# A fused linear-attention and gated-convolution kernel: the first two batches in a hand-written order

## The chip, the cores and the metric

The kernel runs on one core of one Trainium2 chip. Time is device time in microseconds, the median of the runs. A core has five engines that work beside each other: TensorE (PE; its weight loads are shown as PEld), VectorE (DVE), ScalarE (ACT), GpSimd (POOL) and SyncE (SP). Each takes its own instructions in order. Data moves between DRAM and the on-chip memory (SBUF) through 16 DMA engines; matmuls write into a small accumulator memory (PSUM).

## The reference

There are 8 batches, 8 heads, a sequence of 576 and a head dimension of 64. The first half is a linear attention with cosine weights over the position, the second a projection, a long convolution done with a Fourier transform, a product of three terms and an output projection.

```python
q_p, k_p = phi(q), phi(k)       # phi(x) = concat(relu(x) * cos_w, relu(x) * sin_w)
kv  = einsum('bhsf,bhsd->bhfd', k_p, v);  z = sum(k_p, axis=2)
num = einsum('bhsf,bhfd->bhsd', q_p, kv)
den = einsum('bhsf,bhf->bhs', q_p, z)[..., None] + 1e-06
x   = (num / den) with the heads side by side             # (8, 576, 512)
x1, x2, x3 = split(x @ w_proj, 3)                          # w_proj: 512 x 1536
x2_conv = irfft(rfft(x2, axis=1) * rfft(filter_fft, axis=0))
out = (x1 * x2_conv * x3) @ w_out                          # float32
```

## The kernel before

One batch goes through these stages; a name in brackets is the tile that the stage writes, and appears so in the profile.

- `load_qk` reads q, k and v of a batch from DRAM as fp32 and writes them to SBUF as fp16 (`raw`, six buffers in turn; 512 KB and 64 KB for each of q, k, v). GpSimd issues these loads, and those of the weights `wp`, `wo` and of the filter `filt`.
- `emit_phi` makes phi(k) (`kp`) and phi(q) (`qp`) on VectorE (lines 107 and 109, which are helpers). `emit_va` copies v (`va`), on ScalarE (L149) or VectorE.
- `emit_kv` multiplies kp and va on PE (L435) and copies the result (`kvs`).
- `emit_qt` transposes qp into `qpt`. For batches 0 and 1 PE does it, and ScalarE and VectorE each copy one head (L459, L460). From batch 2 on it is four DMA transposes per batch issued by SyncE (L447). There is one `qpt` buffer, so that the transposes of a batch wait for `num` of the batch before.
- `emit_num` multiplies qpt and kvs (L472), and VectorE divides (`rcp`, then `att`, L482).
- `emit_fx` is the first step of the Fourier transform, a matmul over att (L499, L505), copied to `fx` (L510). `emit_xt` transposes att into `xt`: by PE for batch 0, by one DMA transpose on SyncE (L520) for the others.
- `emit_gate` multiplies xt with two thirds of w_proj (L604: 64 matmuls per batch in four chunks), ScalarE copies the two results (L609), VectorE multiplies them (`g`).
- `emit_x2` multiplies fx with the other third (L541, `x2f`), `emit_dft` does the second step of the transform (L580, `xf`) and the product with the filter's spectrum on VectorE (`m`, `yf`), `emit_inv` goes back (L621, L625, `eq`), `emit_y` combines (`eo`, `y`, `ye`), and `emit_out` makes the output (L671, L677), which ScalarE copies (`os`) and SyncE writes to DRAM (L704, L692).

Before batch 0 the kernel makes its tables: GpSimd writes counters (`emit_iotas`), VectorE turns them into columns (`emit_cols`, `emit_rows`), ScalarE takes sines of them (`emit_fwd_tables`, `emit_inv_turns`, `emit_inv_tables`, `emit_h_tables`), and PE makes the filter's spectrum (`emit_h`: hE, hO, hL). `warm_up` issues matmuls whose result is not used.

Batches overlap: a step of the loop `for b in range(1, B + 1)` has x2, dft, gate and inv of batch b, num and fx of batch b+1, the loads of batch b+2, and out of batch b-1. Source order is not the order on the engines: a planner reorders the instructions of each engine, by its own costs and by when buffers come free, and `with behind(key)` puts the instructions of its block behind a marked instruction on the same engine. In the order that it settled on, SyncE issues the transposes `qpt` of batch 2, `xt` of batch 1, `qpt` of batch 3, `xt` of batch 2, the output of batch 0, `qpt` of batch 4, `xt` of batch 3, the output of batch 1, and so on.

Of the kernel before, what the change touches and what calls it, by code (L numbers as in the profile page):

```python
# [17 lines left out]
def kernel(  # L18
# [19 lines left out]
    nc = tc.nc  # L38
# [58 lines left out]
    feo = setupp.tile([NP, 2, 3, DM], FP16, tag="feo", name="feo")  # L97
    qpt_buf = const("qpt", [128, NH, SP_], FP16)
# [33 lines left out]
    def load_qk(b, nm, hs=slice(0, NH)):  # L132
        src = {"q": q, "k": k, "v": v}[nm]
        if hs.start == 0:
            raw_t[(b, nm)] = raw_buf[raw_n[0] % len(raw_buf)]
            raw_n[0] += 1
        rw = raw_t[(b, nm)]
        nc.gpsimd.dma_start(  # L138
            out=rw[:, hs, 0 : 4 * D],
            in_=src[b, hs, 0:NM].rearrange("h (p j) d -> p h (j d)", j=4),  # L140
        )
        nc.gpsimd.dma_start(
            out=rw[0:64, hs, 4 * D : 5 * D], in_=src[b, hs, NM:S].rearrange("h p d -> p h d")
        )

    def emit_va(b, xs=range(4), copy=nc.scalar.copy):
        for x in xs:
            hs = slice(2 * x, 2 * x + 2)
            copy(  # L149
                out=va_buf[b % 2][:, hs, :, 0:D],  # L150
                in_=raw_t[(b, "v")][:, hs].rearrange("p h (j d) -> p h j d", j=NJ),
            )

    def emit_input_dma(b):
        load_qk(b, "q")
        load_qk(b, "k")
        load_qk(b, "v")
# [23 lines left out]
    def emit_iotas(part):  # L181
        if part == 0:
            iota("s4_i", [128, NJ], lambda t: [
                (t[:, 0:4], [[1, 4]], 0, 4), (t[0:64, 4:5], [[1, 1]], NM, 1),
                (t[64:128, 4:5], [[1, 1]], 0, 1),
            ])
            iota("p_i", [128, 1], lambda t: [(t, [[1, 1]], 0, 1)])
            iota("kr_i", [128, 4, 2], lambda t: [(t, [[1, 4], [0, 2]], 1, 0)])
            iota("nrow_i", [128, 128], lambda t: [(t, [[1, 128]], 0, 0)])
            iota("er_i", [128, 4, 16], lambda t: [(t, [[1, 4], [4, 16]], 0, 0)])  # L190
            return
# [11 lines left out]
    def emit_cols():  # L203
# [7 lines left out]
        for r in raw_buf[0:3]:  # L211
            nc.vector.memset(r[64:128, :, 4 * D : 5 * D], 0.0)
# [32 lines left out]
        for r in raw_buf[3:]:  # L245
            nc.vector.memset(r[64:128, :, 4 * D : 5 * D], 0.0)
# [56 lines left out]
    def emit_fwd_tables():  # L303
# [14 lines left out]
        frac(tn)  # L318
        sin_of(fsin, tn[:, 0:288])
# [9 lines left out]
    def emit_inv_tables():  # L329
        tn, mk = cc["tn_inv"], cc["mk"]  # L330
        frac(tn)
        sin_of(itab[:, 3:6].rearrange("p a b -> p (a b)"), tn[:, 0 : 3 * QS])
        cos_of(itab[:, 0:3].rearrange("p a b -> p (a b)"), tn[:, QS : 4 * QS])
        for c in range(NC):
            for par in range(2):
                tsc(itl[:, c, :, par], itab[:, 2:4], mk[:, 2 * c + par : 2 * c + par + 1], AL.mult)

    def emit_h_tables():
# [8 lines left out]
        tnf = tn.rearrange("p a b -> p (a b)")  # L347
        frac(tnf)
        sin_of(hs_.rearrange("p a b -> p (a b)"), tnf)
        cos_of(hc.rearrange("p a b -> p (a b)"), tnf)  # L350

        hb = cc["hb"] = setupp.tile([NP, 3, 3, 32], FP16, tag="hb", name="hb")
# [6 lines left out]

    def emit_h(bls):  # L360
        hc, hs_, hb = cc["hc"], cc["hs"], cc["hb"]
        fa = filt16.rearrange("p x (j n) -> p x j n", j=3)
        for x, op in ((0, AL.add), (1, AL.subtract)) if 0 in bls else ():
            with behind("phi", 1, "k"):
                nc.vector.tensor_tensor(
                    out=feo[:, x].rearrange("p j n -> p (j n)"),
                    in0=filt16[:, 0], in1=filt16[:, 1], op=op,
                )
# [29 lines left out]
    def emit_phi(b, nm, h0=0, nh=NH):  # L398
        rw = raw_t[(b, nm)]
        dst = kp_t if nm == "k" else qp_t  # L400
        if nm == "k":
            if h0 == 0:
                dst[b] = work.tile([128, NJ, NH, 2, D], FP16, tag="kp", bufs=1, name=f"kp{b}")
            t = dst[b]
            for j in range(NJ):
# [37 lines left out]
    def emit_qt(b, hp):  # L443
        qp, qpt = qp_t[b], qpt_buf
        hsl = slice(2 * hp, 2 * hp + 2)
        if b >= DMA_QT:
            nc.sync.dma_start_transpose(  # L447
# [5 lines left out]
        for hh in range(2):  # L453
            for j in range(NJ):
# [3 lines left out]
                )  # L458
        nc.scalar.copy(out=qpt[:, 2 * hp], in_=u[:, 0, 0:SP_])  # L459
# [29 lines left out]
    def emit_fx(b, cs=range(NC), wm=0):  # L489
# [4 lines left out]
        for c in cs:  # L494
# [15 lines left out]
            mark["fx", b] = nc.scalar.copy(  # L510
# [52 lines left out]
    def emit_dft(b, bls=range(3)):  # L563
# [6 lines left out]
        for bl in bls:  # L570
# [11 lines left out]
            mark["xf", b, bl] = nc.scalar.copy(out=xf, in_=u[:, :, 0:n])  # L582
            m1 = work.tile([128, 2, n], FP16, tag=f"m1{n}", bufs=1, name=f"m1_{b}_{bl}")
# [10 lines left out]
    def emit_gate(b, c):  # L594
        xt = xt_t[b]
        if c == 0:
            moe.setdefault(b, {})["g"] = work.tile([128, NC, S], FP16, tag="g", name=f"g{b}")
# [113 lines left out]
    HA, HB = slice(0, 4), slice(4, 8)  # L711
    load_qk(0, "k", HA)
    emit_iotas(0)
    for nm, hs in (("v", HA), ("q", HA), ("k", HB), ("v", HB), ("q", HB)):
        load_qk(0, nm, hs)
    emit_iotas(1)
    load_wp(0)
    load_wp(2)
    load_wp(1)
    load_qk(1, "q")  # L720
    load_qk(1, "k")
    load_qk(1, "v")
    load_filter()
    load_wo()
    emit_cols()
    emit_warm(1)
    emit_phi(0, "k", 0, 4)
    emit_va(0, (0, 1))
    emit_kv(0, 0)
    emit_phi(0, "q", 0, 4)  # L730
    for hp in (0, 1):
        emit_qt(0, hp)
    emit_num(0, 0, 4)
    emit_num(0, 1, 1)
    emit_phi(0, "k", 4, 4)
    emit_va(0, (2, 3))
    emit_kv(0, 1)
    emit_fx(0, (0, 1))
    emit_xt(0, (0, 1))
    emit_phi(0, "q", 4, 4)  # L740
    for hp in (2, 3):
        emit_qt(0, hp)
    emit_num(0, 2, 1)
    emit_num(0, 3, 1)
    emit_xt(0, (2, 3))
    emit_fx(0, (2, 3), 3)
    emit_rows()
    emit_inv_turns()
    for c in range(NC):
        emit_gate(0, c)  # L750
    emit_fwd_tables()
    with behind("att", 0, 3):
        emit_phi(1, "q")
    for hp in range(4):
        emit_qt(1, hp)
    emit_h_tables()
    with behind("g", 0, 0):
        emit_phi(1, "k")
    with behind("x0s", 0, 2):
        emit_va(1)  # L760
    emit_x2(0, (0,))
    emit_kv(1)
    emit_x2(0, (1,))
    emit_num(1, 0)
    emit_num(1, 1)
    emit_x2(0, (2,))
# [3 lines left out]
    emit_h((0,))  # L770
    emit_dft(0, (0,))
    emit_h((1,))
    emit_dft(0, (1,))
    emit_h((2,))
    emit_dft(0, (2,))
    with behind("kvs", 1):
        emit_inv_tables()
    emit_input_dma(2)
    with behind("qpt", 1, 3):
        emit_phi(2, "q")  # L780
    with behind("att", 1, 1):
        emit_phi(2, "k")
    with behind("x2f", 0, 2):
        emit_va(2)
    for c in range(NC):
        emit_qt(2, c)
    for c in range(NC):
        emit_fx(1, (c,))
    setup_stack.close()
    late["p"] = ctx.enter_context(tc.tile_pool(name="late", bufs=1))  # L790
    emit_x2(1, (0, 1))
    for c in range(NC):
        emit_inv(0, c)
    emit_kv(2)

    for b in range(1, B + 1):
# [16 lines left out]
        if b == 1:  # L813
            for c in range(NC):
                emit_y(0, c)
# [20 lines left out]
        if n + 1 < B:  # L836
            emit_input_dma(n + 1)
            with behind(*(("yf", 0, 2) if b == 1 else ("g", b - 1, NC - 1))):
# [3 lines left out]
            with behind(*("att", n, 3)):  # L842
                emit_phi(n + 1, "k")
            if b == 1:
                with behind("kvs", 2):
                    emit_va(n + 1)
            else:
                with behind("eo", b, 3):
                    emit_va(n + 1, (0, 1))
                with behind("g", b, 0):  # L850
                    emit_va(n + 1, (2, 3), nc.vector.tensor_copy)
# [42 lines left out]
```

## Time and profile before

| | us |
|---|---|
| median of 3 runs (254.1 to 255.73) | 255.11 |
| the profiled execution, its own time | 254.64 |
| its span in the profile | 252.9 |
| PE busy in the span | 216.1 (85%) |
| VectorE busy | 192.7 (76%) |
| ScalarE busy | 168.8 (67%) |
| mean granted PE clock | 0.941 of full speed |

The profile's times are counted from the start of the span. A group of instructions is shown with its line, engine, operation, the tile written and the tiles read, and a count (x40). An engine is idle until a releaser lets it go on: an instruction of another engine, or the landing of a DMA transfer. The granted PE clock is the speed that PE's throttle allows, 1.00 or about half. The DMA share is the mean busy share of the 16 DMA engines; it goes above 1 where packets overlap. "SPq" is SyncE's time on a DMA issue, which is not the time that the data takes: the time to landing is shown apart.

### The profile page before, as it was taken

To read this page: it belongs to the slowest core of one execution; us is meant where nothing else is said; L and a number is where in the kernel's file an instruction comes from. 1 tells how busy PE (TensorE), PEld (TensorE's weight loads), DVE (VectorE), ACT (ScalarE), POOL (GpSimd) and SP (SyncE) were. 2 spreads that over 40 slices of the span, in tenths; PEclk is the share of its full clock that TensorE was granted. 3 is DMA by queue.
4 is the path that set the end of the run, shared out by engine and by line. 5 is a ranking of instruction groups with operands and counts; after the bars stand their busy time and mean duration, and the time that the engine had idled before them with its cause. 6 is when DMAs were issued, how large, how long until landed. Compare 5 with 4: busy or idle time off the path is not lost.

```text
span 252.9 us, 5925 instructions
## 1 busy us (share of the span) xinstructions
PE 216.1 (85%) x2278; PEld 144.4 (57%) x2278; DVE 192.7 (76%) x660; ACT 168.8 (67%) x264; POOL 49.4 (20%) x79
## 2 busy tenths in 40 slices
PE   0379799989421899999999999999999999999980
PEld 0358577556210586668557855776586658635830
DVE  7589868799819159897979798978996694727751
ACT  2246999997512377478858876796679577767821
POOL 8992364523220002202220220000000000000000
PEclk9995999999755699999999999999999999999998
DMA  5999999999999999999999999965940531053015
GB/s 60 148 194 203 191 205 192 192 173 133 175 140 179 178 150 196 255 135 163 171 278 166 184 158 274 194 136 186 210 108 0 189 83 23 14 177 141 25 25 187
DMA packets 95613, 39.13 MB, mean 155 GB/s; under 512 B 63648, under 2 KB 91296, under 8 KB 95584
## 3 DMA queue, kind: packets, MB, share of 16 engines
q0 software_dynamic: 40064, 16.85, 54.6%
q1 hardware_dynamic: 55152, 21.31, 45.7%
q10 hardware_dynamic: 368, 0.59, 0.7%
q8 instruction: 18, 0.29, 0.5%
q14 instruction: 11, 0.09, 0.1%
HBM read 33.69 MB, written 9.44 MB: 171 GB/s over the span
## 4 chain that ended last, share of the span: by engine, by line
PE 64%; DMA 19%; ACT 9%; DVE 4%; POOL 2%; issue 1%; ACTq 0%; POOLq 0%
PE x L604 23%; PE out L671 11%; PE x L541 10%; DMA xt<-att 7%; DMA raw<-in_v_dram 5%; DMA qpt<-qp 4%; PE dft L580 4%; PE fx L499 3%; PE inv L621 3%; PE kv L435 3%; PE inv L625 3%; DMA raw<-in_k_dram 3%; ACT x2f L559 2%; DVE kp L109 2%; PE out L677 2%; PE fx L505 1%
## 5 line engine op out<-in xcount | busy, mean ns | idle before, releaser
L604 PE MATMUL x<-xt,wp 128*128 128x288 f16 x512 | 68.9, 291 | 5.9 <-DMA xt<-att 5.9
L604 PEld LDWEIGHTS <-wp 128*128 128x128 f16 x512 | 50.1, 99 | 21.4 <-DMA xt<-att 6.8
L541 PE MATMUL x<-wp,fx 128*128 128x512 f16 (+1 forms) x160 | 35.7, 388 | 0.8 <-DVE qpt L460 0.6
L559 ACT ACTIVATE x2f<-x 128x1024 f16<-128x1024 f32 (+1 forms) x24 | 21.0, 881 | 21.7 <-PE x L541 21.7
L671 PE MATMUL out<-wo,y 128*128 128x512 f16 x128 | 29.6, 379 | 2.5 <-ACT os L699 2.5
L611 DVE TENSOR_TENSOR g<-x0s,x2s 128x576 f16<-128x576 f16 x32 | 14.5, 453 | 20.5 <-ACT x2s L609 20.3
L609 ACT CAST x2s<-x 128x576 f16<-128x576 f32 x32 | 20.5, 640 | 11.3 <-PE x L604 11.3
L609 ACT CAST x0s<-x 128x576 f16<-128x576 f32 x32 | 20.6, 645 | 10.8 <-PE x L604 9.2
L482 DVE TENSOR_TENSOR att<-num,rcp 128x640 f16<-128x640 f32 x32 | 26.2, 822 | 0.6
L472 PE MATMUL num<-kvs,qpt 128*128 128x65 f16 x320 | 15.1, 198 | 10.7 <-DMA qpt<-qp 7.6
L472 PEld LDWEIGHTS <-qpt 128*128 128x128 f16 x320 | 13.0, 100 | 17.3 <-DMA qpt<-qp 8.6
L582 ACT CAST xf<-dft 128x1024 f16<-128x1024 f32 (+1 forms) x24 | 19.1, 802 | 4.8 <-PE dft L580 4.1
L541 PEld LDWEIGHTS <-fx 128*128 128x128 f16 (+1 forms) x160 | 12.6, 100 | 16.0 <-issue 3.3
L510 ACT CAST fx<-fx 128x576 f16<-128x576 f32 x32 | 20.3, 653 | 1.4 <-PE fx L505 1.4
L149 ACT COPY va<-raw 128x640 f16<-128x640 f16 x24 | 16.6, 746 | 6.2 <-DMA raw<-in_v_dram 6.2
L671 PEld LDWEIGHTS <-y 128*128 128x128 f16 x128 | 12.2, 98 | 14.2 <-issue 1.1
L138 POOL DMA_DIRECT2D raw<-in_k_dram x9 | 8.6, 954 | 52.9 <-DVE kp L109 50.2
L642 DVE TENSOR_TENSOR eo<-eq 128x288 f16<-128x288 f16 x64 | 17.7, 299 | 1.3 <-ACT eq L631 1.2
L631 ACT CAST eq<-inv 128x576 f16<-128x576 f32 x32 | 18.3, 672 | 0.0
L435 PE MATMUL kv<-va,kp 128*128 128x65 f16 x320 | 12.6, 198 | 6.1 <-ACT va L149 6.1
L702 ACT ACTIVATE os<-out 128x1024 f32<-128x1024 f32 x14 | 14.6, 1039 | 4.9 <-PE out L671 4.1
L109 DVE TENSOR_SCALAR kp<-raw,ccol 128x512 f16<-128x512 f16 (+1 forms) x45 | 16.9, 376 | 1.2 <-DMA raw<-in_k_dram 1.2
(154 smaller groups left out, 400.3 us busy)
## 6 DMA issues: line engine op xcount, KB each, us to landing
out_dram<-os SPq DMA_DIRECT2D x30, 256.0 KB, 3.4
raw<-in_q_dram POOLq DMA_DIRECT2D x7, 512.0 KB, 13.5
raw<-in_k_dram POOLq DMA_DIRECT2D x7, 512.0 KB, 13.4
raw<-in_v_dram POOLq DMA_DIRECT2D x7, 512.0 KB, 15.9
wp<-in_moe_w_proj_dram POOLq DMA_DIRECT2D x3, 512.0 KB, 8.6
out_dram<-os SPq DMA_DIRECT2D x15, 64.0 KB, 3.8
filt<-in_moe_filter_fft_dram POOLq DMA_DIRECT2D x2, 288.0 KB, 12.8
raw<-in_k_dram POOLq DMA_DIRECT2D x2, 256.0 KB, 5.3
```

What stands on the lines that cost most here:

```text
L109: return nc.vector.tensor_scalar(out=out, in0=in0, scalar1=s1, scalar2=s2, op0=op0, op1=op1)
L435: nc.tensor.matmul(u[:, h // 4, ds((h % 4) * 65, 65)], kp[:, j, h].rearrange("p a b -> p (a b)"), va[:, h, j, 0:65], start=(j == 0), stop= ...
L472: nc.tensor.matmul(u[:, hh, ds(t * 65, 65)], qpt_buf[:, h, ds(t * 128, 128)], kvs[:, h // 4, ds((h % 4) * 65, 65)], start=True, stop=True,)
L482: mark["att", b, hp] = nc.vector.tensor_tensor(out=att[:, hp].rearrange("p t (h d) -> p h t d", h=2), in0=nv[:, :, :, 0:D], in1=rcp.unsque ...
L510: mark["fx", b] = nc.scalar.copy(out=fx[:, c].rearrange("p (v t a) -> p t v a", t=4, a=16), in_=uf.rearrange("p (t v a) -> p t v a", t=4, ...
L541: nc.tensor.matmul(dst, fx[:, c, ds(128 * ch, n)], wp16[:, c, ds(DM, DM)], start=(c == cs[0]), stop=(c == cs[-1]),)
L559: mark["x2f", b, bl] = nc.scalar.mul(out=x2f[:, 2 * bl : 2 * bl + n], in_=u[:, 0:n], mul=X2SC)
L582: mark["xf", b, bl] = nc.scalar.copy(out=xf, in_=u[:, :, 0:n])
L604: nc.tensor.matmul(u[:, hf, 0:HS], wp16[:, i, ds(w * DM + c * 128, 128)], xt[:, i, ds(HS * hf, HS)], start=(i == 0), stop=(i == NC - 1),)
L609: mark[f"x{w}s", b, c] = nc.scalar.copy(out=x, in_=u[:, :, 0:HS])
L631: mark["eo", b, c] = nc.scalar.copy(out=eq.rearrange("p a b c -> p a (b c)"), in_=u[:, :, 0:HS])
L671: nc.tensor.matmul(u[:, x], y[:, c, ds(QS * t, 128)], wo16[:, c], start=(c == 0), stop=(c == NC - 1),)
```

## The change

Everything from the first instruction to `emit_kv(3)` is put between `manual_schedule()`'s enter and exit; in this stretch each engine gets its instructions in source order, and the source is a long list of calls written out by hand. The loop then starts at b = 2, and the special cases for b = 1 in it are gone. Many helpers are split, so that their VectorE and ScalarE parts can be placed apart (`emit_h_tables`, `emit_h_sines`, `emit_h_left`, `emit_feo`, `emit_fwd_sines`, `emit_inv_left`, `emit_mul`, `js` of `emit_phi`), and some copies change: `qpt` of batch 0 is copied by ScalarE alone, two heads at once; two of four `fx` copies of batch 0 and half of the `va` copies of batches 1 to 3 go to VectorE. `g` gets two buffers.

v of batch 0 is read into `v32`, an fp32 tile in one of the `qp` buffers, by SyncE; its second half waits for the first load of k. The iotas of the first columns go ahead of the first load on GpSimd, and the number of warm-up matmuls becomes 14 and 4. `xt` of batch 1 now stands ahead of `qpt` of batch 2 on SyncE, and `qpt` of batch 3 behind the output of batch 0. The first load of batch 3 (q) waits until the third `qpt` transpose of batch 2 has landed. The batches' buffers in `raw` shift by one, since v of batch 0 uses none.

In the compiled order GpSimd issues, after the weights, q, k, v of batch 1, the filter, q, k, v of batch 2, wo, q of batch 4, and then q, k, v of batch 3, k and v of batch 4, and q of batch 5.

```diff
+    v32 = work.tile([128, NH, NJ * D], FP32, tag="qp", bufs=2, name="v32")
...
-        nc.gpsimd.dma_start(
+        load_rows(nc.gpsimd, rw, src, b, hs, after)
+
+    def load_rows(queue, rw, src, b, hs, after=None):
+        first = queue.dma_start(
             out=rw[:, hs, 0 : 4 * D],
             in_=src[b, hs, 0:NM].rearrange("h (p j) d -> p h (j d)", j=4),
         )
-        nc.gpsimd.dma_start(
+        mark["load", b] = queue.dma_start(
             out=rw[0:64, hs, 4 * D : 5 * D], in_=src[b, hs, NM:S].rearrange("h p d -> p h d")
+        )
+
+        if after:
+            hold(first, after)
+
+    def hold(ins, key):
+
+        tc.add_manual_dep(
+            ins.ins, mark[key].ins.name,
+            mybir.DependencyInfo(mybir.DependencyClass.Sync, mybir.DependencyReason.DATA),
+            reason="hold",
         )
...
-                in_=raw_t[(b, "v")][:, hs].rearrange("p h (j d) -> p h j d", j=NJ),
...
+                in_=(raw_t[(b, "v")] if b else v32)[:, hs].rearrange("p h (j d) -> p h j d", j=NJ),
...
+        if b == 0:
+            nc.scalar.copy(out=qpt[:, hsl], in_=u[:, :, 0:SP_])
+            return
...
+    manual = tc.manual_schedule()
+    manual.__enter__()
+    emit_iotas(-1)
     load_qk(0, "k", HA)
+    mark["k0"] = mark["load", 0]
+    load_rows(nc.sync, v32, v, 0, HA)
     emit_iotas(0)
...
-    load_wo()
     emit_cols()
-    emit_warm(1)
+    emit_warm(14)
     emit_phi(0, "k", 0, 4)
+    load_rows(nc.sync, v32, v, 0, HB, "k0")
     emit_va(0, (0, 1))
     emit_kv(0, 0)
+    emit_warm(4)
...
+    emit_xt(0, (2, 3))
+    emit_fx(0, (0, 1))
+    emit_fx(0, (2, 3), copy=nc.vector.tensor_copy)
+    emit_input_dma(2)
+    load_wo()
+    emit_h_tables()
+    emit_gate(0, 0)
+    emit_h_sines()
+    emit_fwd_tables()
+    emit_gate(0, 1)
+    emit_fwd_sines()
+    emit_phi(1, "q")
+    emit_gate(0, 2)
     emit_inv_turns()
...
+    emit_gate(0, 3)
+    emit_phi(1, "k", js=(0, 1))
     emit_x2(0, (0,))
+    emit_qt(1, 0)
+    emit_qt(1, 1)
...
+    emit_h((0,))
+    emit_phi(2, "q")
     emit_num(1, 0)
     emit_num(1, 1)
...
+    emit_h((1,))
+    frac(cc["tn_inv"])
     emit_num(1, 2)
     emit_num(1, 3)
     emit_xt(1)
...
     emit_h((2,))
...
+    emit_dft(0)
+    emit_inv_tables()
     for c in range(NC):
         emit_qt(2, c)
...
+    emit_fx(1)
+    emit_inv_left()
     setup_stack.close()
     late["p"] = ctx.enter_context(tc.tile_pool(name="late", bufs=1))
+    emit_phi(2, "k")
     emit_x2(1, (0, 1))
...
+    emit_xt(2)
+    for c in range(NC):
+        emit_inv(1, c)
+    emit_out(0, OG[0:1])
+    emit_fx(2, (0, 1))
+    emit_out(0, OG[1:2])
+    emit_fx(2, (2, 3))
+    emit_out(0, OG[2:3])
+    emit_input_dma(3, ("qpt", 2, 2))
+    emit_phi(3, "q")
+    for x in range(4):
+        emit_qt(3, x)
+    emit_phi(3, "k")
+    emit_va(3, (0, 1))
+    emit_va(3, (2, 3), nc.vector.tensor_copy)
+    for c in range(NC):
+        emit_y(1, c)
+    emit_kv(3)
+    manual.__exit__(None, None, None)
-
-    for b in range(1, B + 1):
+    for b in range(2, B + 1):
```

## The prediction

> **What bounds the kernel now.** I read the windows table first (busy time per stretch), then the chain that ended last, then SyncE's own transposes, then the landing times of single transfers. Windows table (stretch and its length, then PE, PEld, DVE, ACT, POOL busy, PE clock, DMA share, GB/s):
>
> ```profile
> 30.00:36.00 6.00, 6.00 (x52) 4.78 (x51) 3.63 (x13) 5.65 (x10) 3.13 (x4) 1.00 1.33 203
> 60.00:66.00 6.00, 4.44 (x86) 3.86 (x84) 5.97 (x22) 4.02 (x7) 2.77 (x3) 1.00 1.46 147
> 66.00:72.00 6.00, 1.71 (x18) 0.71 (x18) 2.47 (x10) 3.61 (x5) 1.56 (x2) 0.51 1.52 144
> 72.00:78.00 6.00, 2.70 (x22) 0.89 (x22) 2.81 (x7) 1.38 (x2) 0.69 (x1) 0.50 1.42 174
> 78.00:84.00 6.00, 1.01 (x5) 0.67 (x6) 4.57 (x14) 0.23 (x1) 0.00 (x0) 0.50 1.40 178
> ```
>
> From 66 to 84 PE works 5.42 of 18 us, at half clock, while DMA is saturated. From 88 on PE is full (131.63 of 132 us up to 220). So the kernel has three parts: a start (PE idle or cold until the gate matmuls begin at 30.62), the hole at 66 to 84, and a PE-bound remainder. The chain names the hole (start, us, what):
>
> ```profile
> 54.34 10.73 DMA qpt<-qp
> 65.07 17.88 DMA xt<-att
> 82.99 3.90 PE x L604 x16
> ...
> 100.65 1.38 PE kv L435 x40
> 102.03 1.73 PE x L541 x8
> ```
>
> SyncE's issues of transposes, early and late:
>
> ```profile
> 46.78 18.23 SPq L447 DMA_TRANSPOSE qpt<-qp  x4
> 65.07 10.25 SPq L520 DMA_TRANSPOSE xt<-att  x1
> ...
> 104.09 11.70 SPq L447 DMA_TRANSPOSE qpt<-qp  x4
> ...
> 153.05 10.00 SPq L447 DMA_TRANSPOSE qpt<-qp  x4
> ...
> 176.51 5.64 SPq L447 DMA_TRANSPOSE qpt<-qp  x4
> 182.25 2.72 SPq L520 DMA_TRANSPOSE xt<-att  x1
> ```
>
> Four qpt transposes hold SyncE 5.64 us when no loads run (landing 3.1 to 3.2 us each), 18.23 us among the loads (landing 10.0 to 15.1 us). The loads they meet are for batches 3 to 5, not needed for 20 to 60 us: issued from 37.3 on, they land at 51 (q3), 57, 64, 70 (q4), 77, 82, 88, 93 (v5).
>
> **What the skill says.** "DMA: Bandwidth & Descriptors", section "Issuing engines are not separate DMA queues": transfers from all issuing engines run on the same 16 DMA engines and interleave; its section "Queues, rings and completion order" adds that an engine goes round-robin between queues, packet by packet. The trace agrees: 3.2 us alone, up to 15.1 us shared. "TensorE: Matmul & The Clock Gate", section "What's actually happening": an idle window of about 3.4 us drops the clock to half. The trace agrees: clock 0.50 in the hole, and the 16 gate matmuls after it take 3.90 us against 1.96 later.
>
> **The change, part by part.**
>
> *v of batch 0 on SyncE.* GpSimd loses two pairs of issues, about 1.5 us each (0.81 + 0.69 for the second half of v0), so its loads start up to 3.0 us earlier; but from 6 us on DMA is saturated (share 1.30 and more), so I take 2 us. v32 is twice the bytes of f16 v: 0.59 MB more, 2 to 3 us at 200 to 260 GB/s: together 0 for the loads (between 2 us earlier and 1 later). Its ScalarE copy from fp32 is not in the trace; "VectorE: DVE Perf Modes", section "The TRN2 errata", prices a ScalarE SBUF copy at 224 cycles plus one per element at 1.2 GHz, 0.72 us for 640; the f16 copy measures 0.73. I take 0.73, no change.
>
> *Start.* The hand order puts VectorE's whole preparation ahead of the first kp. p waits for GpSimd's p_i (3.54 now, about the same after); then memsets 1.5 us, the dependent chain 1.5, tables and four raw memsets 2.8: kp from about 9.4 instead of 5.65, a loss of 3.7. But then nothing breaks the row: 10 kp 2.1, qp 1.5, 10 kp 2.1, qp 1.5, so 16.6 against 20.1 now. att needs ScalarE: the last qpt copy (1280 wide, about 1.3 us each, in a row with va and kvs) ends about 22.7, num(0,3) 23.2, att 24.4, xt copy 26.2, fx on PE 27. Gate starts at 27 against 30.62: 3.6 us gained. The 17 added warm-up matmuls (14+4 against 1 first; 0.22 to 0.4 us each) lie in PE's idle time before kv at 11.5; without that cover they would cost up to 7 us.
>
> *Gate(0) to x2(1).* Now 30.6 to 60.2. I laid the new ScalarE order against the durations: gate copies 8 x 0.54, six sine steps 4.3, tn_inv 1.4 put x2s(0,3) at 39.1; x2f, four qpt, va, kvs, hE, hO, hL, xf, itab (1.6) follow; VectorE (phi 1, feo 1.8, phi 2 q, four att 1.1 each, mul 4.4, itl 1.8, phi 2 k 2.6) reaches 63.6. fx(1)'s copies stand behind itab, to 59.5; x2(1) ends near 63. The 3.6 us won at the start are lost here; nothing hides it, for all three engines are about 90% busy.
>
> *The hole.* att(1,3) ends about 54.7; xt(1) now goes on SyncE ahead of qpt(2), and the loads of batch 3 wait for qpt(2,2). Only v2, wo and q4 (in the compiled order q4 stands ahead of the held q3, so it isn't held) may be left, and by the present 3.1 us per tensor they end about 50 to 54. So xt(1) costs 2.5 to 4.4 us and qpt(2) 5.6: both land by 66, xt(1) by 59 to 61, qpt(2) before num(2) at about 74. The hole is gone. Held q3, k3, v3 land from 68 on, 3.1 us apart, before phi(3) at 80. Behind the held load on GpSimd stand all later loads, of which none is needed before that.
>
> *Then*, PE work after x2(1): gate 4 x 1.96, x2 0.55, inv 2 x 1.9, dft 1.3, kv(2) 1.38, num 1.2, out 4.0, fx(2) 1.6, kv(3) 1.4, which is 23.1; VectorE has 22 (mul 4.4, y 5.6, att 4.4, phi(3) 4.7, g and va 2.9). kv(3) so ends near 88, against 102.03: 14 us ahead.
>
> *New wait.* On SyncE qpt(3) now stands behind xt(2) and the six issues of out(0). Now it goes at 75.4, before xt(2), and is there when num(3) wants it. After: out(0) ends on PE about 85, its last issue about 87, so qpt(3,0) goes at 87.5 and num(3,0) is due at 90. Its cost: at the least 3.2 us landing and 1.4 apart: num(3,3) at about 94. At present qpt directly behind the out issues needs longer: issued 104.09, the last lands at 119; issued 153.05, the last at 166.3: 13 to 15 us. I take 14: 101.5, num(3,3) done at 102, against 107.1 now. What follows is the same PE-bound work. Sum: 107.1 - 102 = 5.1 us net of 14. The profiled run is 254.64 (span 252.9 and 1.7 around it), 0.47 under the median 255.11: 254.64 - 5.1 = 249.5.
>
> **Rivals.** *A: the new wait is short.* For it: transposes alone land in 3.2 us, and the hold thins the loads. Against: out(0)'s 1.2 MB lie ahead in the same queue. num(3,3) at 94, 13 us gained: 241.6.
> *C: nothing gained.* Bytes are conserved: DMA is saturated to 103 us now, and nearly the same set must have moved before num(3). Holding loads only helps as far as they can go later; q5, k5, v5 are freed by phi(3) and va(3) at 82 to 88. Last landing near 107: 254.6.
> *D: slower.* These three loads (1.77 MB) go exactly when qpt(3) does. From 46.8 to 74.6 the four qpt (1.31 MB) had 47 GB/s beside loads at about 98. At that share the loads run to 105; until then 0.85 MB of the queue's 1.9 MB (qpt and half of out) moves, the rest at 230 GB/s by 109.5. num(3,3) at 110, 3 us late, and 2 us more for PE gone cold: 259.6. It decides when the last qpt(3) lands after 107.
> *The order isn't what it says*: excluded for SyncE, PE, VectorE, since the compiled rows show it; for the hold it is true in part (q4).
>
> **Numbers.** Forecast 0.46 (own range 245.5 to 252.5), A 0.30, C 0.12, D 0.12. About 1% (2.5 us) is what a measurement can tell from no change. Faster 0.76, same 0.12, slower 0.12. Range 241 to 256: it leaves out D and the lower part of A.
>
> **What would show it.** Right: no transpose in the chain between 54 and 83; first gate matmul at about 27; xt(1) landing in under 7 us; num of batch 3 waiting for DMA qpt, with qpt(3) issued after out(0), at 85 to 90; windows PE-full from about 102. Wrong: gate starting after 30; PE empty before x2(1), with ScalarE or VectorE as releaser; num(3) without a wait (A), or waiting past 107 (D); a second starved stretch after 110, since all transposes now follow later loads.

## The result and the profile after

The changed kernel takes 276.13 us (median of 4; 275.25 to 277.15) against 254.61 for the kernel before beside it: a ratio of 1.084, interval 1.078 to 1.090. The forecast was 249.5. Some executions of e1, e14 and e15 below took over 1.5% longer than the fastest of the same kernel, and their times and ratios leave these out. The profiled execution has a span of 273.4 us against 252.9, so 20.5 us have to be found.

The windows table of the kernel after (stretch and its length, then PE, PEld, DVE, ACT, POOL busy, PE clock, DMA share, GB/s):

```profile
48.00:54.00 6.00, 5.06 (x85) 3.40 (x83) 5.90 (x18) 3.00 (x4) 1.26 (x2) 1.00 0.01 3
...
66.00:72.00 6.00, 6.00 (x58) 3.96 (x56) 2.10 (x7) 4.88 (x9) 4.67 (x7) 1.00 0.96 136
72.00:78.00 6.00, 5.75 (x94) 4.54 (x86) 3.62 (x7) 5.33 (x10) 3.16 (x5) 1.00 1.55 185
78.00:84.00 6.00, 3.86 (x61) 3.20 (x59) 5.69 (x23) 2.12 (x4) 0.00 (x0) 1.00 1.58 189
84.00:90.00 6.00, 4.88 (x29) 3.05 (x29) 5.72 (x20) 2.55 (x4) 0.00 (x0) 0.72 0.49 55
90.00:96.00 6.00, 4.82 (x44) 3.07 (x43) 5.93 (x19) 4.24 (x7) 2.21 (x1) 1.00 0.59 146
...
102.00:108.00 6.00, 0.00 (x0) 0.00 (x0) 0.52 (x3) 0.00 (x0) 0.88 (x1) 0.62 1.50 165
108.00:114.00 6.00, 0.97 (x15) 0.81 (x16) 2.90 (x11) 0.00 (x0) 0.00 (x0) 0.50 1.42 176
114.00:120.00 6.00, 3.54 (x17) 1.35 (x15) 0.55 (x3) 1.02 (x1) 0.69 (x1) 0.75 1.64 119
120.00:126.00 6.00, 2.30 (x28) 1.28 (x28) 1.02 (x3) 1.01 (x1) 0.00 (x0) 0.54 1.39 162
126.00:132.00 6.00, 6.00 (x45) 2.90 (x43) 4.83 (x10) 2.71 (x4) 0.00 (x0) 0.61 1.06 213
```

The hole at 66 to 84 is gone, as forecast: PE works 15.61 of these 18 us, against 5.42 before. A worse one stands at 102 to 126, where PE works 6.81 of 24 us. And there is something that the kernel before doesn't have between 6 and 160 us: DMA that stands idle, at 48 to 54 (3 GB/s) and for most of 84 to 90 (55 GB/s). GpSimd's issues of loads say why: it waits for VectorE (phi of q, in the helper at L110) to free a buffer of `raw`.

```profile
52.56 0.89 POOL L142 DMA_DIRECT2D raw<-in_q_dram  x1 [17.97 <-DVE qp L110]
...
93.80 3.55 POOL L142 DMA_DIRECT2D raw<-in_q_dram  x1 [17.87 <-DVE qp L110]
```

The first is q4, the second q5; behind the first, q3 waits for the hold.

The chain that ended last names the new hole (start, us, what):

```profile
98.76 1.31 PE x L574 x6
100.07 1.45 SPq L477
101.61 23.74 DMA qpt<-qp x2
125.40 0.73 PE num L505 x10
```

TensorE's matmuls of num(3), with the idle time before them and what ended it in brackets:

```profile
109.60 0.73 PE L505 MATMUL num<-kvs,qpt 128*128 128x65 f16 x10 [9.54 <-DMA qpt<-qp]
113.76 0.73 PE L505 MATMUL num<-kvs,qpt 128*128 128x65 f16 x10 [3.43 <-DMA qpt<-qp]
120.53 0.73 PE L505 MATMUL num<-kvs,qpt 128*128 128x65 f16 x10 [2.98 <-DMA qpt<-qp]
125.40 0.73 PE L505 MATMUL num<-kvs,qpt 128*128 128x65 f16 x10 [3.17 <-DMA qpt<-qp]
```

The last of them ends at 126.1. In the kernel before, the last ten of num(3) were these, without a wait:

```profile
106.66 0.48 PE L472 MATMUL num<-kvs,qpt 128*128 128x65 f16 x10
```

They ended at 107.1, so this is 19.0 of the 20.5 us. From there to the end both kernels need nearly the same (147.3 and 145.8). SyncE's timeline (start, us, what it issued) shows when these transposes went (the last line holds qpt(3) and qpt(4)):

```profile
57.67 2.54 SPq L553 DMA_TRANSPOSE xt<-att  x1
60.33 6.15 SPq L477 DMA_TRANSPOSE qpt<-qp  x4
91.75 2.50 SPq L553 DMA_TRANSPOSE xt<-att  x1
94.43 1.91 SPq L745 DMA_DIRECT2D out_dram<-os  x4
96.44 1.23 SPq L733 DMA_DIRECT2D out_dram<-os  x2
97.78 31.18 SPq L477 DMA_TRANSPOSE qpt<-qp  x8
```

qpt(2), issued at 60.33, landed in 3.6 to 3.8 us each. qpt(3), issued at 97.78, landed in 11.8 to 14.6 us each, the last at about 125.4: 27.6 us for the four, as long as qpt(2) took in the kernel before (46.8 to 74.4). Beside it the landing times show q5 (issued 93.8, 11.9 us), k5 (98.3, 13.3), v5 (99.9, 19.3) and q6 (102.4, 22.4). The hole was moved by one batch and is not gone.

### The profile page after: what moved, and what is told of

Same layout as the page of the kernel before. It is cut to its first block, busy times and chain, and to the rows that moved or that the text cites. A ratio compares the mean times of both kernels' runs of the same rounds, so it can differ in the third digit from the quotient of the medians.

```text
span 273.4 us, 5930 instructions
## 1 busy us (share of the span) xinstructions
PE 222.1 (81%) x2282; PEld 145.6 (53%) x2282; DVE 198.4 (73%) x665; ACT 165.7 (61%) x256; POOL 48.0 (18%) x75
## 4 chain that ended last, share of the span: by engine, by line
PE 57%; DMA 15%; DVE 13%; ACT 11%; issue 2%; SPq 1%; POOL 0%; DVEq 0%; ACTq 0%; POOLq 0%
PE x L645 20%; PE x L574 10%; PE out L712 9%; DMA qpt<-qp 9%; PE dft L613 3%; DMA v<-in_v_dram 3%; PE kv L465 3%; DVE att L515 3%; PE fx L532 3%; ACT x2f L592 2%; PE inv L662 2%; PE inv L666 2%; DMA raw<-in_k_dram 2%; PE num L505 2%; PE out L718 1%
## 5 line engine op out<-in xcount | busy, mean ns | idle before, releaser
L645 PEld LDWEIGHTS <-wp 128*128 128x128 f16 x512 | 50.4, 100 | 16.4 <-issue 3.4
L574 PE MATMUL x<-wp,fx 128*128 128x512 f16 (+1 forms) x160 | 39.0, 410 | 2.2 <-ACT fx L543 1.7
L505 PE MATMUL num<-kvs,qpt 128*128 128x65 f16 x320 | 15.7, 203 | 23.7 <-DMA qpt<-qp 19.1
L712 PE MATMUL out<-wo,y 128*128 128x512 f16 x128 | 30.6, 387 | 2.6 <-ACT os L740 2.3
L652 DVE TENSOR_TENSOR g<-x0s,x2s 128x576 f16<-128x576 f16 x32 | 14.6, 455 | 22.0 <-ACT x2s L650 22.0
L511 DVE TENSOR_TENSOR rcp<-num,epsc 128x10 f32<-128x10 f32 x32 | 5.1, 161 | 25.9 <-PE num L505 25.6
L574 PEld LDWEIGHTS <-fx 128*128 128x128 f16 (+1 forms) x160 | 13.5, 105 | 19.5 <-issue 6.8
L712 PEld LDWEIGHTS <-y 128*128 128x128 f16 x128 | 12.4, 99 | 15.1 <-issue 2.1
L142 POOL DMA_DIRECT2D raw<-in_q_dram x9 | 10.5, 1163 | 54.5 <-DVE qp L110 39.0
L662 PE MATMUL inv<-itab,yf 128*128 128x144 f16 x128 | 16.9, 232 | 2.8 <-DVE att L515 2.8
L543 ACT CAST fx<-fx 128x576 f16<-128x576 f32 x30 | 18.7, 647 | 0.0
L465 PE MATMUL kv<-va,kp 128*128 128x65 f16 x320 | 13.2, 197 | 5.1 <-DVE kp L110 1.9
## 6 DMA issues: line engine op xcount, KB each, us to landing
raw<-in_q_dram POOLq DMA_DIRECT2D x7, 512.0 KB, 11.8
```

Source lines behind the costliest of these rows:

```text
L465: nc.tensor.matmul(u[:, h // 4, ds((h % 4) * 65, 65)], kp[:, j, h].rearrange("p a b -> p (a b)"), va[:, h, j, 0:65], start=(j == 0), stop= ...
L505: nc.tensor.matmul(u[:, hh, ds(t * 65, 65)], qpt_buf[:, h, ds(t * 128, 128)], kvs[:, h // 4, ds((h % 4) * 65, 65)], start=True, stop=True,)
L543: mark["fx", b] = copy(out=fx[:, c].rearrange("p (v t a) -> p t v a", t=4, a=16), in_=uf.rearrange("p (t v a) -> p t v a", t=4, a=16)[:, : ...
L574: nc.tensor.matmul(dst, fx[:, c, ds(128 * ch, n)], wp16[:, c, ds(DM, DM)], start=(c == cs[0]), stop=(c == cs[-1]),)
L645: nc.tensor.matmul(u[:, hf, 0:HS], wp16[:, i, ds(w * DM + c * 128, 128)], xt[:, i, ds(HS * hf, HS)], start=(i == 0), stop=(i == NC - 1),)
L662: nc.tensor.matmul(u[:, comp, ds(par * QS, QS)], yf[par][:, comp, ds(c * 128, 128)], itab[:, par + 4 * comp], start=(par == 0), stop=False,)
```

## The experiments

The theory after the comparison: the wait of num(3) is made by the loads of batches 5 and 6, which take the DMA engines while qpt(3) is on its way (rival D of the prediction, mis-sized). The rivals to it: the place of qpt(3) on SyncE's queue behind xt(2) and out(0) (the step of the forecast), and the hold on batch 3's loads.

**e1_hold5.** The loads of batches 5 and 6 wait until the third qpt(3) has landed. The hold here covers both parts of q, k and v; for batch 3 that changes nothing, since its k and v stood behind the held q on GpSimd anyway.

```diff
         if after:
             hold(first, after)
+            hold(mark["load", b], after)
...
-        load_qk(b, "k")
-        load_qk(b, "v")
+        load_qk(b, "k", after=after)
+        load_qk(b, "v", after=after)
...
-            emit_input_dma(n + 1)
+            emit_input_dma(n + 1, ("qpt", 3, 2) if n + 1 in (5, 6) else None)
```

> The changed kernel, with the loads of batches 5 and 6 held until the third qpt transpose of batch 3 has landed. Contention theory (the four qpt of batch 3 take 27.6 us because q, k, v of batch 5 and q of batch 6 run beside them): the four land within 6 to 9 us of the first issue at about 97.8, num of batch 3 ends near 107 instead of 126, and the time falls by 17 to 20 us to 256 to 259. Queue theory (they are late because they stand behind the output writes on SyncE's queue, loads or not): 270 or more.

Measured 265.30 us, ratio to the kernel before 1.045 (1.039 to 1.052). TensorE's waits of num(3), and the one that comes next:

```profile
98.92 0.48 PE L506 MATMUL num<-kvs,qpt 128*128 128x65 f16 x10 [1.32 <-DMA qpt<-qp]
100.47 0.54 PE L506 MATMUL num<-kvs,qpt 128*128 128x65 f16 x10 [1.07 <-DMA qpt<-qp]
...
133.96 3.17 PE L646 MATMUL x<-xt,wp 128*128 128x288 f16 x16 [2.08 <-DMA xt<-att]
```

Behind the same stores in the same queue, qpt(3) now lands in 3.4 to 5.4 us and num(3) ends at 106.5. The queue isn't the cause of the long wait; the loads beside it are. But of the 19.6 us that num(3) is earlier only 10.8 are left at the end: q5 goes only from 104, and then qpt(4) takes up to 13.9 us and xt(3) 17.9. The time lies above the 256 to 259 that contention alone was expected to give.

**e13_fewer_bytes.** This kernel leaves out the large load of q, k and v of batches 5 and 6.

```diff
-        first = queue.dma_start(
+        first = b in (5, 6) or queue.dma_start(
```

> Kernel after that leaves out the large load (512 KB) of each of q, k and v of batches 5 and 6, so these two batches are computed from the values that batches 3 and 4 left in the buffers; every other instruction and its order is kept. Theory (bytes of these loads make qpt(3) late, and bytes held back come due later, which is why e1 gave half back): num(3) ends at 104-109 and not at 126.1, nothing is given back, 246-257 us. Rival (queue order or the issue itself): num(3) ends at 120 or later, 268 us or more.

Measured 256.7 us, ratio 1.012 (1.006 to 1.019). num(3):

```profile
101.35 1.52 PE L505 MATMUL num<-kvs,qpt 128*128 128x65 f16 x20 [4.61 <-DMA qpt<-qp]
106.07 0.76 PE L505 MATMUL num<-kvs,qpt 128*128 128x65 f16 x10
107.93 0.48 PE L505 MATMUL num<-kvs,qpt 128*128 128x65 f16 x10
```

It ends at 108.4 and nothing is given back: 19.4 of the 21.5 us are gone once these bytes are, as the theory expected. So e1's missing half was the bytes themselves, due later. And with some 3 MB less to write into its buffers the hand order is still no faster than the kernel before.

**e4_no_hold** takes the hold off batch 3.

```diff
-    emit_input_dma(3, ("qpt", 2, 2))
+    emit_input_dma(3)
```

> The changed kernel without the hold on the loads of batch 3. Contention theory: q, k, v of batch 5 are freed by the computation on batch 3, not by the hold, so the long wait of num of batch 3 stays; 272 to 278. If the hold itself pushed the loads into that window, the time falls to 255 to 262.

Measured 274.39 us, ratio 1.080 (1.074 to 1.086), in the range of the contention theory: it isn't the hold. The idle stretch only moves:

```profile
84.00:90.00 6.00, 3.48 (x26) 2.42 (x26) 5.73 (x20) 2.27 (x4) 0.00 (x0) 0.83 0.01 3
```

Without the hold DMA runs on at 48 to 54 (132 GB/s), the last load lands at 80.1 and nothing moves up to 93, since all six raw buffers are full: phi(3,q), phi(3,k) and va(3), which empty them, stand at the end of VectorE's row (q5 waits 20.27 us for phi(3,q)).

**e2_qt3_before_out** sets the loads of batch 3, phi(3,q) and qpt(3) ahead of inv(1) and out(0).

```diff
     emit_xt(2)
+    emit_input_dma(3, ("qpt", 2, 2))
+    emit_phi(3, "q")
+    for x in range(4):
+        emit_qt(3, x)
     for c in range(NC):
         emit_inv(1, c)
...
-    emit_input_dma(3, ("qpt", 2, 2))
-    emit_phi(3, "q")
-    for x in range(4):
-        emit_qt(3, x)
```

> The changed kernel, with phi(q) and the qpt transposes of batch 3 ahead of the output of batch 0 in the source, so ahead of its six issues on SyncE. Contention theory: the first issue comes 3.5 us earlier (94.3), but the loads of batch 5 are there from 93.8; 268 to 273. Queue theory: the wait goes, 256 to 260.

Measured 271.18 us, ratio 1.071 (1.062 to 1.080), in the range of the contention theory. qpt(3) is issued 6 us earlier, at 91.7 (some 3 us of it are there before the edit, see e8), and num(3) ends at 111.6, but num(4) now waits for its qpt in the same way, up to 146.

**e6_phi3_early and e7_phi3_qt3_early** move VectorE's steps on batch 3 to the stretch after kv(2); e7 also sets qpt(3) ahead of xt(2). e7 against the kernel after:

```diff
     emit_kv(2)
+    emit_input_dma(3, ("qpt", 2, 2))
+    emit_phi(3, "q")
     emit_y(0, 0)
...
+    emit_phi(3, "k")
     emit_num(2, 2)
     emit_num(2, 3)
+    emit_va(3, (0, 1))
+    emit_va(3, (2, 3), nc.vector.tensor_copy)
+    for x in range(4):
+        emit_qt(3, x)
     emit_xt(2)
```

(e6 has the same without the two lines of emit_qt, which stay behind out(0); the old places are deleted in both.)

> Kernel after with VectorE's steps on batch 3 (phi(3,q), phi(3,k), its half of va(3)) moved from the end of its row to the stretch after kv(2), so that the raw buffers of batch 3 come free about 10 us earlier; qpt(3) stays where it is, behind xt(2) and the six stores of out(0). Theory (DMA idles at 84-92 because the raw buffers are full, and the loads then collide with qpt(3)): q5, k5 and v5 are issued from about 81 to 92 and not from 94 to 100, qpt(3) lands in 5 to 9 us each, num(3) ends near 108-114 and not 126, and of the 12-18 us about half stays: 264-270 us. Rival (the place of qpt(3) on the SyncE queue, or VectorE's longer row ahead of y(0), makes the wait): num(3) ends at 123 or later, 273-279 us.

> As e6_phi3_early, and the four issues of qpt(3) moved ahead of xt(2) as well. Theory of contention: the first issue is near 91, beside k5 and v5; landings 6-11 us, num(3) ends at 104-112, xt(2) lands later by about 6 us and gate(2) may wait for it; 262-270 us. Rival (the place on the queue decides): num(3) ends at 98-102, no wait for qpt(3), 252-258 us.

e6: 269.96 us, ratio 1.059 (1.051 to 1.067); e7: 261.83, ratio 1.025 (1.015 to 1.034), so slower than the kernel before, but not surely by 2%. e6 is divided. Its time lies at the upper edge of the theory's range, and qpt(3) lands in 4.8 to 7.5 us as the theory had it; but num(3) ends at 123.1, which is the rival's figure. q5 does go at 82, but k5 only at 95, because phi(3,k) has to wait for its place in a full VectorE row. That longer row puts xt(2) off from 91.75 to 98.12, xt(2) then takes 14.6 us beside k5, q6 and v5, and so out(0) and, at 109.68, qpt(3) are late. In e7 qpt(3) goes before all that, from 81.75, num(3) doesn't wait and ends at 106.6; the time is just under the range of the theory and above that of the rival. What is left is one wait of TensorE's gate matmuls:

```profile
114.23 3.42 PE L645 MATMUL x<-xt,wp 128*128 128x288 f16 x16 [6.35 <-DMA xt<-att]
```

xt(2), now behind qpt(3) and beside k5, q6 and v5, took 16.4 us to land.

**e10_early_no_hold** is e7 without the hold.

```diff
-    emit_input_dma(3, ("qpt", 2, 2))
+    emit_input_dma(3)
```

> As e7_phi3_qt3_early, and without the hold of batch 3's loads. Theory (idle transfer time before 110 us is what is paid for later; e7 still idles at 42-54): if the loads of batch 3 move into that gap, less is left for later, and the time is 3 to 8 us under e7's 261.8: 254-259 us. Rival (the loads then share the queues with xt(1) and qpt(2) and the hole of the kernel before comes back at 60-80): 261-270 us. If q of batch 4, first on GpSimd's queue, still waits for phi(2,q) until 52 us, nothing moves: 261-263 us.

Measured 262.21 us, ratio 1.032 (1.025 to 1.039): the same as e7, and the theory's 254 to 259 is missed. The gap at 42 to 54 is filled (195 and 178 GB/s), the old hole doesn't come back, and a gap at 72 to 84 opens (102 and 37 GB/s), since the buffers are full again until phi(3,q), for which q5 waits up to 80.7.

**e14_early_hold5** is e7 with all loads of batches 5 and 6 held, as in e1, until xt(2) has landed.

```diff
-            emit_input_dma(n + 1)
+            emit_input_dma(n + 1, ("xt", 2) if n + 1 in (5, 6) else None)
```

> As e7_phi3_qt3_early, and all loads of batches 5 and 6 held until xt(2) has landed. Theory (what e7 still loses, 6.35 us of gate(2) waiting for xt(2), is transfers sharing the queues, and the bytes held come due later): xt(2) lands in 4-8 us and not 16.4, gate(2) doesn't wait, but qpt(4), xt(3) or qpt(5) are late, so that half or more comes back: 257-263 us. Rival (only this collision is left between the hand order and the kernel before, and there is room for the bytes later): 250-255 us.

Measured 263.50 us from two executions, ratio 1.035 (1.027 to 1.042). TensorE's waits:

```profile
132.46 0.48 PE L506 MATMUL num<-kvs,qpt 128*128 128x65 f16 x10 [2.82 <-DMA qpt<-qp]
140.91 3.59 PE L646 MATMUL x<-xt,wp 128*128 128x288 f16 x16 [5.70 <-DMA xt<-att]
```

xt(2) lands in 4.1 us instead of 16.4 and nobody waits for it; one batch later num(4) and the gate wait in its place. The time is 1.7 us above that of e7, with intervals that overlap, and just above its expected range: the collision was moved again, and nothing was gained.

**e3_before_hold and e9_before_hold3** go the other way: the kernel before, scheduler's order and all, with one part of the change alone. e3 holds the loads of batches 3 and 4 until qpt(2,2) has landed, e9 those of batch 3 only. As in e1 the hold is on both parts of q, k and v (left out here).

```diff
-            emit_input_dma(n + 1)
+            emit_input_dma(n + 1, ("qpt", 2, 2) if n + 1 in (3, 4) else None)
```

> The kernel before, with only this added: all loads of batches 3 and 4 wait until the third qpt transpose of batch 2 has landed. Contention theory: qpt of batch 2 and xt of batch 1 land by about 60, the gate matmuls of batch 1 begin at 63 to 68 instead of 83; 240 to 246, unless the held loads then meet qpt of batch 3. Conservation theory (the bytes have to move anyway, the wait only moves to batch 3): 252 to 257.

> Kernel before with one part of the change alone: all loads of batch 3 (not those of batch 4) held until qpt(2,2) has landed. Theory of contention: xt(1) and qpt(2) no longer share the queues with loads, the hole of TensorE at 66-83 shrinks; batch 4's loads come in order behind batch 3's on the same queue, so most of what e3 gained is here: 247-250 us. Rival (batch 4's loads go ahead and take the place, or the gain of e3 came from batch 4): 252-256 us.

e3: 247.18 us, ratio 0.973 (0.968 to 0.978), faster than both kernels, and 1.2 us above the range of the contention theory. Its SyncE timeline:

```profile
45.93 6.31 SPq L458 DMA_TRANSPOSE qpt<-qp  x4
52.30 2.56 SPq L531 DMA_TRANSPOSE xt<-att  x1
64.78 15.94 SPq L458 DMA_TRANSPOSE qpt<-qp  x4
```

qpt(2) takes 6.31 us of the queue and not 18.23, qpt(3) goes at 64.8 and not at 75.4, and num(3) ends at 97.1. qpt(3) meets loads here too and takes 24.7 us to its last landing, but it goes early enough that num(3) doesn't wait. Between 6 and 150 us the DMA share is never under 0.97. e9: 252.97, ratio 0.994 (0.991 to 0.997), a gain of 0.6%, outside the 247 to 250 of the theory and in the range of the rival. The loads of batch 4, not held, go ahead of the held ones and take their place: SyncE's qpt(2) again needs 15.91 us, q3 is issued at 63.26, and VectorE, whose next step is phi(3,q), stands still with num(2)'s division behind it:

```profile
72.60 1.08 DVE L107 TENSOR_SCALAR qp<-raw 128x2560 f16<-128x2560 f16 x1 [12.47 <-DMA raw<-in_q_dram]
```

**e11_hold_phi3q_later and e15_hold_to_qpt0** try to better e3, in which num(2,3) still waits 3.78 us for VectorE. e11 puts phi(3,q) behind num(2)'s last division; e15 releases the loads at the first landing of qpt(2).

```diff
-            with behind(*(("yf", 0, 2) if b == 1 else ("g", b - 1, NC - 1))):
+            with behind(*(("att", 2, 3) if b == 1 else ("g", b - 1, NC - 1))):
```

```diff
-            emit_input_dma(n + 1, ("qpt", 2, 2) if n + 1 in (3, 4) else None)
+            emit_input_dma(n + 1, ("qpt", 2, 0) if n + 1 in (3, 4) else None)
```

> As e3_before_hold (the kernel before with all loads of batches 3 and 4 held until qpt(2,2) has landed), and phi(3,q) set behind the last division of num(2) in VectorE's row, so that the division doesn't stand behind a wait for q of batch 3. Theory: the wait of num(2,3) for VectorE (3.78 us in e3) goes; qpt(3) comes 1-2 us later and isn't waited for: 243-247 us. Rival (transfers set the time): as e3, 246-249 us.

> As e3_before_hold (the kernel before with the loads of batches 3 and 4 held), released by the first landing of qpt(2) and not the third. Theory (transfers set the time; a hold costs as much idle transfer time as it leaves): q of batch 3 lands some 3 us earlier, VectorE's wait ahead of num(2,3) shrinks from 3.78 us, and qpt(2) and xt(1) land later by 1-3 us: 245-249 us. Rival (all of qpt(2) has to go alone): 249-254 us.

e11: 256.64 us, ratio 1.008 (1.005 to 1.011), 9.5 us worse than e3 and a clear miss. Its VectorE and SyncE timelines say why:

```profile
80.24 0.82 DVE L107 TENSOR_SCALAR qp<-raw 128x2560 f16<-128x2560 f16 x1
```

```profile
45.24 6.39 SPq L458 DMA_TRANSPOSE qpt<-qp  x4
51.68 29.93 SPq L531 DMA_TRANSPOSE xt<-att  x2
83.84 13.27 SPq L458 DMA_TRANSPOSE qpt<-qp  x4
```

The order that the scheduler settled on puts phi(3,q) not 1 or 2 us later but at 80.24 instead of 62.09 (num(2)'s last division ends at 74.6). qpt(3) goes as soon as phi(3,q) is done, at 83.84 instead of 64.78; xt(2), which now stands ahead of it (the second xt of the line x2), has left the queue at 81.6 and isn't what holds it. num(3) waits for qpt(3) (2.12, 1.87 and 4.55 us) and ends at 107.3. So e11 doesn't test the small step that it was meant for. e15: 253.69, ratio 1.000 (0.997 to 1.004): the theory is missed, the hold's gain is gone, and the time lies in the range of the rival, that all of qpt(2) has to go alone. q3, issued at 50.9 beside the last qpt(2), lands in 10.8 us (8.2 in e3), that qpt in 11.0 (3.2 to 3.9 in e3), and xt(1) in 20.3 (7.5).

**The start: e8_v0_no_wait and e12_before_v32.** e8 lets v's second half of batch 0 go at once; e12 is the kernel before with v of batch 0 as fp32 on SyncE.

```diff
-    load_rows(nc.sync, v32, v, 0, HB, "k0")
+    load_rows(nc.sync, v32, v, 0, HB)
```

```diff
+        if (b, nm) == (0, "v"):
+            nc.sync.dma_start(
+                out=v32[:, hs, 0 : 4 * D],
+                in_=src[b, hs, 0:NM].rearrange("h (p j) d -> p h (j d)", j=4),
+            )
...
-                in_=raw_t[(b, "v")][:, hs].rearrange("p h (j d) -> p h j d", j=NJ),
+                in_=(raw_t[(b, "v")] if b else v32)[:, hs].rearrange("p h (j d) -> p h j d", j=NJ),
```

> Kernel after without the wait of v's second half of batch 0 for the first load of k. Theory (this wait held va, and behind it the qpt copies on ScalarE): v lands 2-4 us before 16.4, gate(0) starts at 27.0-28.5 and not 29.89, but the gain is given back since transfers set the time up to 160 us: 273.5-276.5 us. Rival (the start is on the path that sets the end): 272.5-274, as much less as gate(0) is earlier. Rival (v then delays k): gate(0) at 30 or later.

> Kernel before with v of batch 0 alone read as fp32 by the SyncE queue, as the change does it, without the wait for k and without the hand order. What I had priced at about zero for the loads: gate(0) starts within 2 us of 30.62 and the time is 252-257 us. Rival (v as fp32 writes twice the bytes and delays k and q of batch 0): gate(0) at 33 or later, 257-262 us. Rival (GpSimd's queue is relieved and the start is on the path): gate(0) at 27-28, 250-252 us.

e8: 273.71 us, ratio 1.074 (1.066 to 1.082). v lands at 10 and not at 16.4, and the last qpt copy of ScalarE ends 3.3 us earlier, at 20.9, but gate(0) starts at 28.93 against 29.89 in the kernel after: the third division to att now stands in VectorE's row behind some twenty small table steps (20.2 to 22.9). num(3) ends 2.0 us earlier and the kernel is about 2.4 us faster; the two expected ranges overlap, and this run doesn't decide between them. Nor can single profiles carry such differences: in runs with the same start gate(0) is read at 29.13 (e13) to 30.85 (e4), and e1, e2 and e13, which differ from the kernel after only later, begin the gate of batch 1 at 63.6 to 64.5 against 66.9, with a PE clock of 1.00 from 24 to 36 against 0.86.

e12: 262.05, ratio 1.031 (1.026 to 1.035), at the upper end of the range of the rival that v delays k. But that isn't what sets its time. k did land later (7.1 us from issue against 4.2), yet VectorE waits for something else:

```profile
13.16 0.19 DVE L244 RECIPROCAL epsc<-ccol 128x5 f32<-128x5 f32 x1 [8.48 <-ACT ccol L215]
```

The scheduler set ScalarE's copies of v, which wait for v, ahead of the sine for ccol, which every kp needs. k is there from 9.5 on and the first kp comes at 14.3. So e12 prices an order, not the load; the load alone stays unmeasured.

**All runs in one table.** GB/s and PE busy time are those of the stretch 42 to 96 us of each profile; "num(3) done" is the end of its last matmul, "rest" the span after it.

| kernel | GB/s | PE busy | num(3) done | rest | median us |
|---|---|---|---|---|---|
| e3 (before, loads 3 and 4 held) | 180 | 47.22 | 97.1 | 147.2 | 247.18 |
| e9 (before, loads 3 held) | 167 | 36.85 | 106.2 | 145.6 | 252.97 |
| e15 (e3, released early) | 161 | 40.53 | 104.4 | 146.1 | 253.69 |
| before | 168 | 38.66 | 107.1 | 145.8 | 254.4 |
| e11 (e3, phi(3,q) late) | 172 | 43.90 | 107.3 | 146.5 | 256.64 |
| e13 (after, fewer bytes) | 146 | 43.05 | 108.4 | 145.4 | 256.7 |
| e7 (after, phi(3), qpt(3) early) | 142 | 41.69 | 106.6 | 153.3 | 261.83 |
| e12 (before, v as fp32) | 159 | 36.66 | 112.8 | 146.2 | 262.05 |
| e10 (e7, no hold) | 151 | 41.71 | 105.5 | 153.4 | 262.21 |
| e14 (e7, loads 5 and 6 held) | 139 | 41.82 | 106.2 | 157.0 | 263.50 |
| e1 (after, loads 5 and 6 held) | 147 | 43.05 | 106.5 | 156.7 | 265.30 |
| e6 (after, phi(3) early) | 126 | 41.72 | 123.1 | 145.8 | 269.96 |
| e2 (after, qpt(3) earlier) | 139 | 43.05 | 111.6 | 157.6 | 271.18 |
| e8 (after, v0 at once) | 139 | 43.05 | 124.1 | 148.0 | 273.71 |
| e4 (after, no hold) | 125 | 44.72 | 126.2 | 146.7 | 274.39 |
| after | 131 | 43.95 | 126.1 | 147.3 | 276.13 |

Two things are to be read from it. The rest is 145 to 148 us, or 153 to 158 where a transfer is late once more after num(3). And every order with the hand-written start moved 125 to 151 GB/s in this stretch against 168 before, although TensorE was ahead of before in all of them: for the kernel after 54 us x 37 GB/s, 2.0 MB less. By an estimate from its hole (155 GB/s at 102 to 126) these take 12.9 us, and the hole costs 17.2 us of PE's time. A lower rate goes, roughly, with a longer time, but a table of different orders shows the link, not the cause. What e1 and e13 show is that the loads of batches 5 and 6 make the long wait of num(3). That the idle DMA before it is what put them there is not shown: e10 fills the first gap, another opens, and nothing is gained.

## Why the prediction was wrong

*v of batch 0 on SyncE*: nothing in the kernel after speaks against "about 0": v of batch 1, last of its loads, is there at 32.4 against 34.1 before. k lands later (6.1 us from issue against 4.2), but kp waits for VectorE's row anyway and starts at 9.73 (forecast 9.4).

*Start*: gate(0) at 27 forecast, 29.89 measured. A term left out is the wait of v's second half for the first load of k; it lands at 16.4, and ScalarE's row stood behind it:

```profile
16.44 0.73 ACT L164 CAST va<-v 128x640 f16<-128x640 f32 x1 [2.95 <-DMA v<-in_v_dram]
```

The prediction gives this wait no time. But it isn't the whole 2.9 us: without it (e8) the gate starts 1 us earlier, no more than profiles of the same start differ by. The other row that I had too short is VectorE's, where the table steps stand ahead of the third att.

*Gate(0) to x2(1)*: near 63 forecast, the main part of x2(1) ends at 67.1 measured: 2.9 us come from the start, and the other 1.2 are less than profiles of the same start differ by.

*The hole*: right in its mechanism: no transpose in the chain between 54 and 83, xt(1) in 5.3 us, qpt(2) in 3.6 to 3.8, q4 ahead of the hold. The landings are 2 to 6 us later than forecast (xt(1) at 63.0, the last qpt(2) at 68.6, q3 at 73.8), and the wait of q4 for a free buffer, with DMA idle from 46.7 to 52.6, has no term.

*Then*: kv(3) at 88 forecast, 98.75 measured. Here the first large error lies. Some 4 us of it were there at x2(1). For the rest, I took PE's 23.1 us and VectorE's 22 as two rows running side by side. They run one after the other at first. VectorE's timeline:

```profile
70.50 0.46 DVE L652 TENSOR_TENSOR g<-x0s,x2s 128x576 f16<-128x576 f16 x1 [3.61 <-ACT x2s L650]
...
74.06 0.69 DVE L628 TENSOR_TENSOR m<-xf,hE 128x1024 f16<-128x1024 f16 x1 [2.35 <-ACT xf L615]
...
91.63 0.82 DVE L108 TENSOR_SCALAR qp<-raw 128x2560 f16<-128x2560 f16 x1
```

It has 5.72 us to do in the 12 from 66 to 78, then it is full (23.34 of 24 us) up to 102. phi(3,q) so comes at 91.63, although its q is there since 74.2, and everything that hangs on it is late: qpt(3), and the raw buffers for q5, k5 and v5.

*New wait*: the step that decided. "I take 14" us from the first issue of qpt(3) to its last landing, from how qpt goes behind the out stores at 104 and at 153 in the kernel before; it was 27.6. That place in the old profile was the wrong likeness: there one load at a time was on its way beside the transposes (q6 to 114.1; the last load, v7, to 159.8), and here there were up to four. The third row behind out stores, which I passed over, already took longer:

```profile
128.23 14.46 SPq L447 DMA_TRANSPOSE qpt<-qp  x4
```

Its last landing is at 148.2, 19.9 us after the first issue, with two loads beside it at first (v6 to 134.6, q7 to 140.2). The right row stood in the same timeline, qpt(2) at 46.8, 27.6 us among three to five loads (not 27.8: its last landing is at 74.4, and that of the row at 153 at 166.1 and not 166.3; neither changes a sum), and I used it only for rival D. So the same place behind the stores took 13 to 20 us, by what else was on its way. The stores of out(0), on which I had put the wait, landed in 2.5 to 5.9 us, and in e1, with the loads held, qpt(3) behind the same stores took 10.0 us from first issue to last landing. The sum: num(3) at 102 forecast, 126.1 measured; of the 24.1 us, 10.3 are the later issue (97.78 against 87.5) and 13.6 the slower landing. Two signs that I had set for being wrong came true: num(3) waited past 107, and a second starved stretch came, at 102 to 126.

*The rivals.* D had the mechanism: the loads of batch 5 are set free by the same VectorE steps that set qpt(3) free, so the two meet wherever that row ends. Its size was wrong: I let three loads run to 105, and it was four that ran to 124.8 (q6, issued at 102.4, took 22.4 us), since phi(4,q), 97.2 to 102.1, freed the next buffer. With the measured end of num(3) its sum gives 254.64 + 19.0 = 273.6 and not 259.6. C, bytes conserved, had a part of the reason: "Holding loads only helps as far as they can go later" stands in the prediction at 0.12, and e1 and e14 are two cases of it. The Trainium skill's "DMA: Bandwidth & Descriptors", section "Issuing engines are not separate DMA queues", was cited for the old hole (3.2 us alone, up to 15.1 shared) and not applied to the new place of qpt(3), where the trace shows 3.4 to 5.4 (e1, held) against 11.8 to 14.6.

What stays open: what v as fp32 costs by itself (e12 changed an order too), whether the idle DMA of the hand order is what makes its loads collide later, and whether a hand order exists that beats e3; e7, the best of those tried with all bytes, is 14.7 us behind it.

## What to carry to other kernels

When a change takes a transfer out of contention, look for the place where those bytes go instead, and take the price of a transfer from a row with the same neighbours, not from the row with the same queue. An order that is better for the compute engines can empty the load buffers later; here DMA was idle first and its loads collided with transposes afterwards. Moving the steps that free a buffer forward won 6 us here (e6), and 14 with qpt(3) set ahead too (e7), but what stood behind them in the row came later. A hold on loads has to cover all loads that could go past it (e9), and to last until the transfers that it protects are nearly through (e15).

## What the runs showed that I had not expected

- A hold is worth its exact end. Released at the first of four transposes instead of the third (50.9 against 53.3 us for the first load), the last transpose took 11.0 us instead of 3.2, the next xt 20.3 instead of 7.5, and 6.5 us of total time went (e15 against e3).
- Setting one VectorE step behind another that ends at 74.6 put it, in the order that the scheduler then settled on, at 80.2 instead of 62.1, and cost 9.5 us (e11 against e3).
- Four transposes of a batch (1.31 MB) took 27.6 us among loads both at 98 in the kernel after and at 47 in the kernel before, 47 GB/s; that the two agree so well makes no rule, for qpt(3) among loads took 22.5 us in the kernel before and 24.7 in e3.
